# Attention units of a transformer block read in one transfer each: e stored by sign, numerators read with a stride

## The chip, the cores and the metric

The kernel runs on one core of one Trainium2 chip. The metric is device time in microseconds (us) of one execution, lower is better. A core has five engines with queues of their own: PE (TensorE, matrix products; its weight loads are listed as PEld), DVE (VectorE), ACT (ScalarE), POOL (GpSimd) and SP (SyncE, which here only issues transfers). Transfers between device memory (DRAM) and the on-chip memory SBUF run on 16 DMA engines; SP issues most of them, ACT issues one kind. PE writes its results to PSUM banks, 128 partitions of 512 floats.

## The reference

One transformer block on x of 2048 tokens by 1024 features, all in float32:

```python
qkv = x @ wqkv                                  # x after a layer norm; 32 heads of 32
pq = einsum("bhsd,hdf->bhsf", q, w_phi);  pk = einsum("bhsd,hdf->bhsf", k, w_phi)
phi_q = concat([softmax(pq), softmax(-pq)], -1) # 64 features per head; phi_k likewise
kv = einsum("bhsf,bhsd->bhfd", phi_k, v);  z = einsum("bhsf->bhf", phi_k)
num = einsum("bhqf,bhfd->bhqd", phi_q, kv)
den = einsum("bhqf,bhf->bhq", phi_q, z)[..., None] + 1e-6
h = x + (num / den).reshape(B, S, D) @ wo
h2 = h + relu(layernorm(h) @ w1) @ w2           # w1: 1024 x 3584
```

So for every token and head there are 32 exponentials with the sign plus and 32 with the sign minus, called e below.

## The kernel before

**Stages.** The order of all work is written out by hand: a list of PE items (`items`), and for every other step a number (`when(step, f, ...)`), a step being one eighth of an item at first and one quarter later. Each engine carries out its part in the order in which the code issues it. First come keys and values (to about 520 us), with the query projections of tokens 0 to 1023 in between; then the query projections of tokens 1024 to 2047, the attention and the output projection side by side (to about 800 us); then the MLP in a form that needs seven instead of eight block products. Products of matrices are three matmuls each (`mm3`, L182 to L184), since every operand is split in a high and a low part; the weights' split (L125 on ACT, L129 on DVE or POOL) runs beside.

**From the projection to e.** For a tile t of 128 tokens and one half s of the heads, PE leaves pq in a bank. DVE takes the largest and smallest value of each head (L516, L517) and the two differences (L520, L521) into the tile `qe`, 128 tokens by `(a, s, c, f)`: 4 groups of heads, 2 signs, 4 heads, 32 features, 1024 floats. ACT takes the exponential (`q_second`, L525) and stores the tile to the scratch tensor `ed` in DRAM (L527, a transfer on ACT's queue). DVE sums e per head and sign (L533), POOL multiplies sums and inverses to factors `smq` (L543), which SP stores to `smd` for every group of four tiles (`sm_store`, L547).

**Groups and units.** The 16 tiles form four groups of four (`groups`); `place_of` gives a tile's group b and place i in it. For each group there are 8 units, one for each of 8 groups of 4 heads, 32 units in all. A unit is a tile of 128 partitions by 8 x 128 floats (`qe` again in the names of the profile, `xl` for the first six): partitions 32a to 32a + 31 hold 32 tokens t; quarters a = 0, 1 are the signs of tiles i = 0, 1, quarters 2, 3 those of tiles i = 2, 3. The free dimension is `(n, c, f)`: 8 blocks of 32 tokens, 4 heads, 32 features. `at_load` (and, earlier and once more, `early_load` for the first six, whose denominators are made ahead) reads it by `by_quarter` (L551), four transfers of 128 KB on SP's queue, one for each quarter, in pieces of 512 bytes. `sm_load` reads the factors the same way.

**In a unit.** POOL multiplies e by z (L595), DVE sums (L602), ACT copies each quarter's sums to the other sign's quarter (L613), POOL and DVE make the denominator (L617, L618, L621), POOL scales e (L631; L626 for the early units), and DVE turns the tile in blocks of 32 x 32 (`at_turn`, L637): afterwards the partitions are features and the free dimension is `(n, c, t)`, tokens last.

**Numerators.** `at_num` (L650) runs for every second unit: for two units j, two row halves g of 64 partitions (each holds both signs of two tiles) and four heads c, a matmul of `kvL` (64 x 32, stationary) and 256 columns, the turned rows of one head. The eight matmuls of a unit use eight 64 x 32 tiles of the array. f32 matmuls show in the profile as two records each. A row half has its own bank; ACT copies it to the high part of `oT` (L657), DVE takes the low part (L667, `at_low`). `oT` holds for each unit 512 tokens in the order of the tiles and is the stationary operand of the output projection (`wo_item`).

**Two other places the prediction looks at.** `far_scale` (L776), once, at 823 us: 16 small matmuls whose stationary operand is `ident.rearrange("p (t g) -> p g t", g=4)[:, g]`, 32 columns that lie four floats apart. `far_swap` (L781): a DVE turn of 128 x 1024 whose output steps four floats. The transfers `hs<-xin` (L760) store 256 KB in pieces of 512 bytes.

Of the kernel before, what the change touches and what calls it, by code (L numbers as in the profile page):

```python
# [9 lines left out]
F32 = mybir.dt.float32  # L10
# [5 lines left out]
P = 128  # L16
# [124 lines left out]
def kernel(  # L141
# [12 lines left out]
    v, act, pool, pe, sp = nc.vector, nc.scalar, nc.gpsimd, nc.tensor, nc.sync  # L154
# [5 lines left out]
    dram = ctx.enter_context(tc.tile_pool(name="scratch", bufs=1, space=bass.MemoryType.DRAM))  # L160
# [9 lines left out]
    def ac_bank():  # L170
        return psum.tile([P, 512], F32, name="ac", bufs=2)
# [22 lines left out]

    groups = (0, 1, 4, 5), (2, 3, 6, 7), (8, 9, 10, 11), (12, 13, 14, 15)
    place_of = {t: (b, i) for b, tiles in enumerate(groups) for i, t in enumerate(tiles)}
    ed = [dram.tile([8, 4, P, 256], F32, name=f"ed{b}") for b in range(4)]
    smd = [dram.tile([4, P, 64], F32, name=f"smd{b}") for b in range(4)]
    hd = [dram.tile([P, D], F32, name=f"hd{t}") for t in range(NT)]


# [219 lines left out]
    e_of, v_of, phi_of, kv_ps, kd_of = {}, {}, {}, {}, {}  # L421
# [102 lines left out]
    def q_second(s, t):  # L524
        act.activation(e_of[s, t], e_of[s, t], AF.Exp)  # L525
        b, i = place_of[t]
        act.dma_start(ed[b].rearrange("a i p x -> p a i x")[:, 4 * s:4 * s + 4, i, :],  # L527
                      e_of[s, t].rearrange("p a s c f -> p a (s c f)"))

    def q_third(s, t):  # L530
        b, i = place_of[t]
# [12 lines left out]
                               op=ALU.mult)  # L544

    def sm_store(b):
        sp.dma_start(smd[b].rearrange("i p x -> p i x"), smq[:, b % 2].rearrange("p i s n -> p i (s n)"))  # L547

    def by_quarter(dst, src):
        for a in range(4):  # L550
            sp.dma_start(dst[32 * a:32 * (a + 1)],  # L551
                         src[2 * (a // 2):2 * (a // 2) + 2].rearrange("i (n t) (s x) -> s t (i n) x", t=32, s=2)[a % 2])

    def sm_load(b):
        by_quarter(smx[:, b % 2], smd[b])


    e_q, ez_of, tz_of, den_of, ph_of, acc_of, phT_of = {}, {}, {}, {}, {}, {}, {}
# [4 lines left out]
    def at_load(u):  # L563

        e = ap_.tile([P, D], F32, name="qe", bufs=6)
        e_q[u] = e = e.rearrange("p (n x) -> p n x", n=8)
        by_quarter(e, ed[u // 8][u % 8])
# [4 lines left out]
    def early_load(u):  # L572
        e_q[u] = e = xlp.tile([P, D], F32, name="xl").rearrange("p (n x) -> p n x", n=8)
        by_quarter(e, ed[u // 8][u % 8])
# [59 lines left out]
    def at_turn(u):  # L634

        ph = ph_of.pop(u)
        v.transpose(ph, ph)  # L637
        phT_of[u] = ph.rearrange("p (n c t) -> p n c t", n=8, c=4)

    def at_num(u):  # L640


        acc_of[u] = banks = ac_bank(), ac_bank()
        for j in range(2):
            b, q, r = UNITS[u - 1 + j]
            for g in range(2):
                rows = slice(64 * g, 64 * (g + 1))
                for c in range(4):
                    h = 2 * c + r
                    pe.matmul(banks[g][32 * c:32 * (c + 1), 256 * j:256 * (j + 1)],  # L650
                              kvL[rows, 2 * q + h // 4, 32 * (h % 4):32 * (h % 4 + 1)],
                              phT_of[u - 1 + j][rows, :, c, :], start=j == 0, stop=j == 1)
        del phT_of[u - 1], phT_of[u]
        if u % 8 == 1:
            oT[b] = opool[b % 2].tile([P, 2, 8, 512], F32R, name="oT")
        for g in range(2):
            act.activation(at_out(u, 0, g), at_in(banks[g]), AF.Copy)  # L657

    def at_in(ps):
        return ps.rearrange("p (u n) -> p u n", u=2)  # L660

    def at_out(u, part, g):
        return oT[u // 8][:, part, u % 8 - 1:u % 8 + 1, 256 * g:256 * (g + 1)]

    def at_low(u):
        for g, ps in enumerate(acc_of.pop(u)):
            v.tensor_sub(at_out(u, 1, g), at_in(ps), f32(at_out(u, 0, g)))  # L667

    oT, opool = {}, {}
# [277 lines left out]
    def item(gen, *args, keys):  # L947
        items.append((gen, args + (keys,)))
        steps.extend((k,) for k in keys)
        return len(items) - 1  # L950
# [11 lines left out]
    for b, tiles in enumerate(groups):  # L962
        for hf in range(2):

            pairs = b == 0 and hf == 0
            for j in range(0, 4, 2 if pairs else 1):
# [3 lines left out]
                for half in range(2):  # L970
                    n = item(wo_pair, tiles[j:j + 2], hf, half, keys=[("wo", hf, 4 * half + k // 2) for k in range(8)])
# [36 lines left out]
    for t in range(1, NT):  # L1008
        n = t - 1 if t < HT else q_n[1, t - HT] + 1
# [106 lines left out]
    for (sl, t), n in q_n.items():  # L1116
        when(8 * n + 14, q_second, sl, t)
        when(8 * n + 19, q_third, sl, t)
        when(8 * n + 27, q_fourth, sl, t)
        b, i = place_of[t]  # L1120
        if (sl, i) == (1, 3):
            when(8 * n + 34, sm_store, b)
            when(8 * n + (48, 48, 48, 72)[b], sm_load, b)
    for u in range(32):
        start = 8 * (a0 + u) if u >= 8 else 8 * (last_kv + 4) + 19 * u // 2
        slack = 6 if u < 6 else 0

        for step, f, *args in ((-5, at_load), (6, at_sums, 0), (10, at_reduce, 0), (9, at_sums, 1), (12, at_reduce, 1),
                               (14, at_cross), (16, at_den), (18, at_inverse), (20, at_scale), (26, at_turn)):
            if u >= EARLY or f in (at_load, at_scale, at_turn):  # L1130
                when(max(start + step, 8 * (last_kv + 4)), f, u, *args)
        if u % 2:
            when(start + 30 + slack, at_num, u)
            when(start + 32 + slack, at_low, u)
        if u < EARLY:
            start = 8 * (kv_n[1, u // 2, NT - 1] + 4) + (-2, 19)[u % 2]
            for step, f in ((0, early_load), (9, early_sums), (14, early_reduce), (17, at_cross), (20, at_den), (22, early_scale)):
                when(start + step, f, u)
# [73 lines left out]
    for b in range(2):  # L1212
        for m in DOWN:
            n = down_n[b, m, NP - 1] + 1
            name, more = {1: "x1", 5: "x4", 6: "x2", 4: "x3"}.get(m), \
# [109 lines left out]
```

## Time and profile before

| | |
|---|---|
| median of 3 runs | 1880.37 us (1880.06 to 1882.46) |
| the profiled execution | 1877.44 us |
| its span, first to last instruction | 1875.6 us |
| PE busy | 1859.8 us, 99% |
| PE clock granted, mean | 0.999 |
| DVE, ACT, POOL busy | 57%, 41%, 52% |

The profile is of one execution. Rows of groups give line, engine, operation, names as out<-in, the tile of the array for PE, shapes, count, then busy time in us and mean ns of one, then idle time of the engine just before and what ended it. Rows of a timeline start with the start in us and the duration; an x32 is that many instructions merged. Rows of transfers give the count, KB of each and the median us from issue to landing. PEld are weight loads, which overlap with PE; "SPq" and "ACTq" are the sequencers that issue transfers.

### The profile page before, as it was taken

How to read it: one execution, taken by the hardware profiler on the slowest of the kernel's cores; microseconds unless marked ns; L12 is line 12 of the kernel's file. 1: busy time of each engine (PE TensorE's matmuls, PEld its weight loads, DVE VectorE, ACT ScalarE, POOL GpSimd, SP SyncE). 2: the span in 40 equal slices, each digit the busy share in tenths (PEclk: the TensorE clock that was granted, in tenths of full speed). 3: DMA queues.
4: the chain of work that ended last, by engine and by line, in shares of the span. 5: the costliest groups of instructions: out<-in, count | busy, mean ns of one | idle time of the engine just before them, and what ended most of it. 6: DMA issues, size and time to landing. Idle time of an engine off the chain costs nothing.

```text
span 1875.6 us, 29094 instructions
## 1 busy us (share of the span) xinstructions
PE 1859.8 (99%) x10064; PEld 1517.2 (81%) x10064; DVE 1070.5 (57%) x1655; ACT 771.3 (41%) x1379; POOL 981.3 (52%) x991
## 2 busy tenths in 40 slices
PE   9999999999999999999999999999999999999999
PEld 7877788888887777888888888888888888888887
DVE  7787688677689878565555663344433333343333
ACT  5322244233333333255455554444444444444442
POOL 4887745888946989443332222222344444444443
PEclk9999999999999999999999999999999999999999
DMA  7988788666677897887888975666676777777775
GB/s 229 291 290 286 229 295 261 204 196 199 181 217 193 222 224 200 261 283 227 243 265 265 322 260 176 195 192 217 214 230 214 214 220 239 237 215 218 216 215 178
DMA packets 348963, 433.05 MB, mean 231 GB/s; under 512 B 32272, under 2 KB 219664, under 8 KB 348816
## 3 DMA queue, kind: packets, MB, share of 16 engines
q1 hardware_dynamic: 331920, 414.42, 72.6%
q10 hardware_dynamic: 16896, 16.78, 2.7%
q8 instruction: 79, 1.29, 0.3%
q14 instruction: 68, 0.56, 0.1%
HBM read 293.21 MB, written 137.89 MB: 230 GB/s over the span
## 4 chain that ended last, share of the span: by engine, by line
PE 92%; DMA 2%; DVE 2%; POOL 2%; issue 1%; ACT 0%; SPq 0%; DVEq 0%; POOLq 0%; ACTq 0%
PE mm L182 24%; PE mm L183 23%; PE mm L184 23%; PE ac L182 4%; PE ac L184 4%; PE ac L183 4%; PE tp L182 2%; PE tp L184 2%; PE tp L183 2%; PE tp L246 1%; PE ac L465 1%; DMA qe<-ed 1%; POOL qe L631 1%; DMA ed<-qe 1%; POOL ez L595 0%
## 5 line engine op out<-in xcount | busy, mean ns | idle before, releaser
L129 POOL TENSOR_TENSOR w<-raw,w 128x512 fp32r<-128x512 f32 x353 | 470.1, 1334 | 698.6 <-ACT w L125 651.4
L125 ACT ACTIVATE w<-raw 128x512 fp32r<-128x512 f32 x686 | 409.4, 626 | 510.9 <-PE mm L184 239.8
L129 DVE TENSOR_TENSOR w<-raw,w 128x512 fp32r<-128x512 f32 x333 | 271.6, 816 | 515.0 <-ACT w L125 503.4
L182 PE MATMUL mm<-w,xT 128*128 128x512 f32 x768 | 305.4, 398 | 0.0
L183 PE MATMUL mm<-w,xT 128*128 128x512 f32 x768 | 299.8, 390 | 0.4 <-POOL w L401 0.4
L184 PE MATMUL mm<-w,xT 128*128 128x512 f32 x768 | 299.2, 390 | 0.0
L184 PE MATMUL mm<-hT,w 128*128 128x512 f32 x672 | 261.4, 389 | 0.0
L182 PE MATMUL mm<-hT,w 128*128 128x512 f32 x672 | 261.4, 389 | 0.0
L183 PE MATMUL mm<-hT,w 128*128 128x512 f32 x672 | 261.4, 389 | 0.0
L182 PEld LDWEIGHTS mm<-w,xT 128*128 128x128 f32 x768 | 144.1, 188 | 34.8 <-issue 3.7
L184 PEld LDWEIGHTS mm<-w,xT 128*128 128x128 f32 x768 | 144.2, 188 | 30.7
L363 POOL TENSOR_TENSOR b<-b 128x256 f32<-128x256 f32 x176 | 143.5, 815 | 47.6 <-DMA b<-in_w_dram 31.9
L183 PEld LDWEIGHTS mm<-w,xT 128*128 128x128 f32 x768 | 144.3, 188 | 29.2 <-POOL w L401 1.0
L182 PE MATMUL mm<-w 128*128 128x512 f32 x392 | 152.5, 389 | 0.0
L183 PE MATMUL mm<-w 128*128 128x512 f32 x392 | 152.5, 389 | 0.0
L184 PE MATMUL mm<-w 128*128 128x512 f32 x392 | 152.5, 389 | 0.0
L183 PEld LDWEIGHTS mm<-hT,w 128*128 128x128 f32 x672 | 126.1, 188 | 26.3
L184 PEld LDWEIGHTS mm<-hT,w 128*128 128x128 f32 x672 | 126.1, 188 | 26.2
L182 PEld LDWEIGHTS mm<-hT,w 128*128 128x128 f32 x672 | 126.1, 188 | 26.1
L183 PEld LDWEIGHTS mm<-w 128*128 128x128 f32 x392 | 73.6, 188 | 15.3
L184 PEld LDWEIGHTS mm<-w 128*128 128x128 f32 x392 | 73.6, 188 | 15.3
L182 PEld LDWEIGHTS mm<-w 128*128 128x128 f32 x392 | 73.6, 188 | 15.3
(173 smaller groups left out, 3119.5 us busy)
## 6 DMA issues: line engine op xcount, KB each, us to landing
raw<-t SPq DMA_DIRECT2D x224, 256.0 KB, 3.8
raw<-ad SPq DMA_DIRECT2D x196, 256.0 KB, 3.0
raw<-in_w_dram SPq DMA_DIRECT2D x168, 256.0 KB, 3.1
ad<-c SPq DMA_DIRECT2D x112, 256.0 KB, 3.6
b<-in_w_dram SPq DMA_DIRECT2D x44, 512.0 KB, 6.0
t<-b SPq DMA_DIRECT2D x44, 512.0 KB, 4.8
ad<-s SPq DMA_DIRECT2D x84, 256.0 KB, 3.8
ed<-qe ACTq DMA_DIRECT2D x32, 512.0 KB, 4.3
```

Source lines behind the costliest of these rows:

```text
L125: nc.scalar.activation(w[:, 0, :], raw[1], AF.Copy)
L129: eng.tensor_tensor(out=w[:, 1, :], in0=raw[1], in1=w[:, 0, :].bitcast(F32), op=ALU.subtract)
L182: pe.matmul(ps, a_hi, b_hi, start=first, stop=False, skip_group_check=more)
L183: pe.matmul(ps, a_hi, b_lo, start=False, stop=False, skip_group_check=more)
L184: pe.matmul(ps, a_lo, b_hi, start=False, stop=last, skip_group_check=more)
L246: pe.transpose(pt[:, k, :], xn[:, (4 * j + k) * P:(4 * j + k + 1) * P], ident)
L363: pool.tensor_tensor(out=tsum[*u, *out], in0=tsum[*u, *a], in1=tsum[*u, *b], op=ALU.subtract)
L465: pe.matmul(kv_ps[s][g][32 * i:32 * (i + 1), 0:64], vt[:, 32 * h:32 * (h + 1)], phi[:, 64 * h:64 * (h + 1)], start=first, stop=last)
L631: pool.tensor_tensor(out=e, in0=e, in1=sd[:, :, None].to_broadcast([P, 32, 32]), op=ALU.mult)
```

## The change

The scratch tensors get another layout, so that a unit's rows lie in DRAM as the unit's partitions want them: the row is `(g, s, t)`, half, sign and 32 tokens, and in it follow four tokens n and 128 floats each. Token 4t + n of a tile now stands in partition t, where before it was token 32n + t.

- The store of e (`q_second`) becomes two transfers, one for each sign, of 256 KB each. Each partition writes 4 pieces of 512 bytes a transfer, where it wrote 4 pieces of 1 KB in one.
- The store of the factors (`sm_store`) writes pieces of 128 bytes instead of 256.
- `by_quarter` becomes one transfer over all 128 partitions, two pieces of 2 KB for each: a unit is read by one issue of 512 KB. The read of the factors likewise has pieces of 512 bytes.
- The turned rows are now `(i, n, c, t)` with tokens in the order `(i, t, n)`. `at_num` reads them in that order: four columns n that lie 128 floats apart, then the next t. The number and shape of the matmuls are the same.
- The copies to `oT` write pieces of 128 floats instead of 256, since a row half g now holds the tiles i = g and 2 + g.

All that stands below `q_second` in the file moves by one or two lines in the new kernel (L551 becomes L552).

On SP, in the output projection of the second group, a unit's load stands as one row with four issues (`hd` and `xh` are results and inputs of the output projection):

```order
L714 DMA hd_90<-xh 128x512
L674 DMA xh<-in_x_dram 128x512
L551 DMA qe<-ed_82 32x8x128 x4
L714 DMA hd_91<-xh 128x512
L674 DMA xh<-in_x_dram 128x512
L551 DMA qe<-ed_82 32x8x128 x4
```

The same place in the changed kernel:

```order
L714 DMA hd_90<-xh 128x512
L674 DMA xh<-in_x_dram 128x512
L552 DMA qe<-ed_82 128x2x512
L714 DMA hd_91<-xh 128x512
L674 DMA xh<-in_x_dram 128x512
L552 DMA qe<-ed_82 128x2x512
```

The place of the load among the others is the same; three of its four issues are gone. On ACT, at the last query tiles, before:

```order
L525 ACTIVATE qe<-qe 128x1024
L527 DMA ed_83<-qe 128x4x256
L613 ACTIVATE qden<-qtz 32x32 x4
L657 ACTIVATE oT<-ac 128x2x256 x2
L125 ACTIVATE w<-raw 128x512 x3
```

and after:

```order
L525 ACTIVATE qe<-qe 128x1024
L529 DMA ed_83<-qe 128x4x128 x2
L613 ACTIVATE qden<-qtz 32x32 x4
L657 ACTIVATE oT<-ac 128x4x128 x2
L125 ACTIVATE w<-raw 128x512 x3
```

A second issue stands between the exponential and the copies of a unit's sums. On PE, DVE and POOL no instruction changes its place.

```diff
-    ed = [dram.tile([8, 4, P, 256], F32, name=f"ed{b}") for b in range(4)]
-    smd = [dram.tile([4, P, 64], F32, name=f"smd{b}") for b in range(4)]
+    ed = [dram.tile([8, 2, P, 512], F32, name=f"ed{b}") for b in range(4)]
+    smd = [dram.tile([2, P, P], F32, name=f"smd{b}") for b in range(4)]
...
     def q_second(s, t):
         act.activation(e_of[s, t], e_of[s, t], AF.Exp)
         b, i = place_of[t]
-        act.dma_start(ed[b].rearrange("a i p x -> p a i x")[:, 4 * s:4 * s + 4, i, :],
-                      e_of[s, t].rearrange("p a s c f -> p a (s c f)"))
+        dst = ed[b].rearrange("a i (g s t) (n x) -> s (i g) (t n) a x", g=2, s=2, n=4)
+        for sd in range(2):
+            act.dma_start(dst[sd, i, :, 4 * s:4 * s + 4], e_of[s, t].rearrange("p a s c f -> s p a (c f)")[sd])
...
     def sm_store(b):
-        sp.dma_start(smd[b].rearrange("i p x -> p i x"), smq[:, b % 2].rearrange("p i s n -> p i (s n)"))
+        sp.dma_start(smd[b].rearrange("i (g s t) (n x) -> (t n) (i g s) x", g=2, s=2, n=4),
+                     smq[:, b % 2].rearrange("p i s n -> p (i s) n"))
 
     def by_quarter(dst, src):
-        for a in range(4):
-            sp.dma_start(dst[32 * a:32 * (a + 1)],
-                         src[2 * (a // 2):2 * (a // 2) + 2].rearrange("i (n t) (s x) -> s t (i n) x", t=32, s=2)[a % 2])
+        sp.dma_start(dst.rearrange("p (i n) x -> p i (n x)", i=2), src.rearrange("i q x -> q i x"))
...
         v.transpose(ph, ph)
-        phT_of[u] = ph.rearrange("p (n c t) -> p n c t", n=8, c=4)
+        phT_of[u] = ph.rearrange("p (i n c t) -> p c i t n", i=2, n=4, c=4)
...
                               kvL[rows, 2 * q + h // 4, 32 * (h % 4):32 * (h % 4 + 1)],
-                              phT_of[u - 1 + j][rows, :, c, :], start=j == 0, stop=j == 1)
+                              phT_of[u - 1 + j][rows, c], start=j == 0, stop=j == 1)
...
     def at_in(ps):
-        return ps.rearrange("p (u n) -> p u n", u=2)
+        return ps.rearrange("p (u i n) -> p u i n", u=2, i=2)
 
     def at_out(u, part, g):
-        return oT[u // 8][:, part, u % 8 - 1:u % 8 + 1, 256 * g:256 * (g + 1)]
+        return oT[u // 8][:, part, u % 8 - 1:u % 8 + 1, :].rearrange("p u (i g n) -> p u i g n", i=2, g=2)[:, :, :, g]
```

## The prediction

> **What bounds the kernel now.** I read the page first, then who PE waited for, then a table of stretches over the attention stage, then that stage's matmuls one by one.
>
> ```profile
> span 1875.6 us, 29094 instructions
> PE 1859.8 (99%) x10064; PEld 1517.2 (81%) x10064; DVE 1070.5 (57%) x1655; ACT 771.3 (41%) x1379; POOL 981.3 (52%) x991
> ...
> PE ac L650 <- DVE qe L637: 4.0, 4, 1.7
> PE mm L183 <- DVE w L129: 1.8, 1, 1.8
> ...
> PE tp L246 <- ACT xin L248: 1.5, 1, 1.5
> PE ac L650 <- POOL ez L595: 1.3, 1, 1.3
> ...
> 540.00:600.00 60.00, 58.74 (x365) 45.86 (x364) 57.18 (x84) 22.91 (x40) 39.70 (x48) 1.00 0.70 193
> 600.00:660.00 60.00, 55.43 (x338) 41.40 (x337) 47.67 (x70) 20.66 (x60) 56.44 (x61) 0.97 0.91 234
> 660.00:760.00 100.00, 96.82 (x661) 74.80 (x661) 77.92 (x118) 34.40 (x86) 83.39 (x98) 1.00 0.83 216
> 610.00:615.00 5.00, 4.59 (x37) 2.92 (x26) 2.59 (x4) 2.65 (x6) 3.77 (x8) 0.66 0.75 163
> ```
>
> PE is the bound: 1859.8 of 1875.6 us. What PE does longer adds to the time one for one; what other engines or DMA queues do shorter can give back no more than PE now waits. A row of waits has the total in us, the count, the longest. A row of stretches has, after the stretch's length, the busy time of PE, PEld, DVE, ACT and POOL, then the granted clock, DMA share and GB/s. Nearly all that this change touches lies from 540 to 760 us. PE idles there 1.26 + 4.57 + 3.18 = 9.0 us (length less PE busy), and near 612 us, after several of these waits, the granted clock is 0.66 for one piece of 5 us, worth 5 x 0.34 = 1.7 us. So 10.7 us is all that faster transfers could bring. DVE is busy 57.18 of 60 us in the first piece and POOL 56.44 of 60 in the second: the waits are largely those engines' work, which the change leaves as it is.
>
> **The numerator matmuls (at_num), read with a stride.** They are what PE itself does differently.
>
> ```profile
> L650 PE MATMUL ac<-qe,kvL x512: 372/376/631, 550.5 to 758.2; 64*32 64x256 f32 x171
> L488 PE MATMUL tp<-zacc,ones 128*128 128x512 f32 x8 | 4.1, 590 | 0.0
> 650.96 1.09 PE L650 MATMUL ac<-qe,kvL 64*32 64x256 f32 x32
> ```
>
> There are 512 records of 256 columns, in 16 bursts of 32 (the timeline row is one, 1.09 us). A burst uses eight 64x32 tiles of the array, so each tile runs 32 / 8 = 4 records in a row. Between f32 matmuls of 256 and 512 columns lie 590 - 376 = 214 ns, so a column costs 214 / 256 = 0.84 ns, and a tile's four records stream for 4 x 256 x 0.84 = 0.86 us: the stream, not a fixed cost, fills the burst. Before, a record reads runs of 32 neighbouring floats; after, neighbouring columns are 128 floats (512 bytes) apart. No matmul of this trace reads its moving operand so, but two other operations step through SBUF:
>
> ```profile
> L776 PEld LDWEIGHTS tp<-scx,ident 128*32 128x32 f32 x32 | 0.6, 154 | 0.4 <-issue 0.4
> L465 PEld LDWEIGHTS ac<-kphi,vt 128*32 128x32 f32 x1024 | 15.4, 110 | 8.5 <-issue 6.8 <-DVE ksm L443 0.7 <-DVE kphi L446 0.4
> L488 PEld LDWEIGHTS tp<-zacc,ones 128*128 128x128 f32 x8 | 1.5, 188 | 0.3
> 823.10 0.58 PEld L776 LDWEIGHTS tp<-scx,ident 128*32 128x32 f32 x32 [0.35 <-issue]
> L781 DVE STREAM_TRANSPOSE xin<-xin 128x1024 f32<-128x1024 f32 x4 | 8.0, 2005 | 0.1
> L637 DVE STREAM_TRANSPOSE qe<-qe 128x1024 f32<-128x1024 f32 x32 | 39.3, 1227 | 4.6 <-POOL qe L631 2.7 <-DMA ed<-qe 1.8
> ```
>
> L776 (far_scale) loads 32 columns of `ident` that lie four floats apart, L465 the same shape with neighbours: 154 against 110 ns, so 44 / 32 = 1.4 ns more a column. Neighbouring columns cost (188 - 110) / 96 = 0.81 ns, close to the 0.84 of a matmul column, so the two streams ask SBUF for floats at one pace. DVE's transpose at L781 writes floats four apart: (2005 - 1227) / 1024 = 0.76 ns more for each.
>
> Bounds for a burst. Low end, 0: the stream's pace of one f32 column per 0.84 ns may be slow enough to hide the step; a gain is excluded, since the same columns pass. By DVE's row: 4 x 256 x 0.76 = 0.78 us a burst, 12.4 us for 16. By the weight row: 4 x 256 x 1.4 = 1.43 us, 22.9 us for 16. High end: the four column tiles on the same 64 partitions take turns, each column having its own 0.84 ns: 16 x 256 x 0.84 = 3.44 us instead of 0.86, 2.58 more a burst, 41.3 us for 16. The 32 strided loads of L776 took 0.58 us for 32 x 32 columns, 0.57 ns a column over four column tiles, which speaks against strict turns. I take the weight row: same engine, a read, the same pace, several tiles at once: **+22.9 us**.
>
> [...]
>
> **The copies out of the banks.** ACT L657 and DVE L667 keep 512 elements, written now in pieces of 128 instead of 256. The nearest pair, whole rows against pieces of 32:
>
> ```profile
> L707 DVE TENSOR_TENSOR xh<-mm,xh 128x512 f32<-128x512 f32 x16 | 11.0, 686 | 17.5 <-DMA hs<-s4l 6.6 <-PE mm L184 5.7 <-DMA hd<-xh 5.2
> L704 DVE TENSOR_TENSOR xh<-mm,xh 128x512 f32<-128x512 f32 x16 | 10.7, 679 | 1.3 <-PE mm L184 1.3
> ```
>
> 7 ns each, 32 times, 0.2 us on an engine that isn't PE: nothing either way. The turn itself (L637) is untouched.
>
> **The transfers.**
>
> ```profile
> ed<-qe ACTq DMA_DIRECT2D x32, 512.0 KB, 4.3
> qe<-ed SPq DMA_DIRECT2D x128, 128.0 KB, 4.6
> xin<-in_x_dram SPq DMA_DIRECT2D x19, 512.0 KB, 5.9
> hd<-xh SPq DMA_DIRECT2D x32, 256.0 KB, 4.4
> hs<-xin SPq DMA_DIRECT2D x32, 256.0 KB, 4.1
> smd<-smq SPq DMA_DIRECT2D x4, 128.0 KB, 3.4
> ...
> L527 ACTq DMA_DIRECT2D ed<-qe x32: 366/367/418, 226.5 to 606.0; - x32
> 689.79 1.90 SPq L551 DMA_DIRECT2D qe<-ed  x4
> 561.01 24.54 SPq L551 DMA_DIRECT2D qe<-ed  x20
> 567.43 2.55 POOL L595 TENSOR_TENSOR ez<-qe,zb 128x512 f32<-128x512 f32 x2 [6.28 <-DMA qe<-ed]
> 584.19 1.92 POOL L631 TENSOR_TENSOR qe<-qe,qden 128x1024 f32<-128x1024 f32 x1 [3.38 <-DVE qden L621]
> 731.74 0.76 PE L650 MATMUL ac<-qe,kvL 64*32 64x256 f32 x16 [1.67 <-DVE qe L637]
> ```
>
> Loads: a unit's four issues take SP 1.90 us, one takes about 1.90 / 4 = 0.48, so SP's queue gains 1.4 us a unit, 45 us over 32 units. The data comes hardly earlier: the last quarter lands 3 x 0.48 + 4.6 = 6.0 us after the first issue, a 512 KB load 5.9 us. Queued behind the loads on SP are the weights of wo and the rows of x; the stretch of 24.54 us for 20 issues is SP held back by buffers that aren't free yet, which one issue in place of four doesn't change. POOL's wait of 6.28 us at 567 is for such a load; but a little later POOL waits for DVE (3.38 us before 584), which is busy nearly throughout. So of the load side I count at most what PE's waits hold, and without the stride I would count 3 us of the 10.7, about the wait at 731.74 (1.67) and that for L248 (1.5), which end a stretch where SP, DMA and POOL are all late.
>
> Stores: 32 more issues on ACT, 32 x 0.367 = 11.7 us, half of them after 510 us, beside 20 to 23 us of ACT work in 60. Pieces become 512 bytes: `hs<-xin` has such pieces (256 KB, 4.1 us), `hd<-xh` pieces of 2 KB (4.4 us), so the second half lands about 0.4 us later than the one store did. Bounds for the time: 0, and 0.4 us for each of the 16 tiles stored after 510 us, 6.4 us, if each were on the path. I take 0: none of PE's waits above is put down to a store. The factors' store goes to 128-byte pieces, 1024 for 512: at worst twice its 3.4 us, four times, with SP waiting before the load; 4 x 3.4 = 13.6 us of SP's queue, less than the 45 it gains; 0 on PE.
>
> **What comes back.** A PE that is later meets fewer waits.
>
> ```profile
> 564.72 1.09 PE L650 MATMUL ac<-qe,kvL 64*32 64x256 f32 x32
> 578.88 1.09 PE L650 MATMUL ac<-qe,kvL 64*32 64x256 f32 x32
> 590.89 0.76 PE L650 MATMUL ac<-qe,kvL 64*32 64x256 f32 x16 [1.26 <-POOL ez L595]
> ```
>
> Three bursts lie before the first wait (the first at 550.5, by the row of L650 above), 3 x 1.43 = 4.3 us against 1.26; a burst comes about every 13 us and adds 1.43, and PE's idle time to 660 is 1.26 + 4.57 = 5.8 us in all, so the lag is ahead of the waits. All 10.7 us could go; but DVE's sums of the output projection wait for PE in its queue, ahead of transposes that PE needs, so I count **-8**. Sum: +22.9 - 8 = +14.9 us. The profiled execution took 1877.44 us (span 1875.6); the median of the runs is 1880.37, 2.9 above. On the median: 1880.4 + 14.9 = 1895 us.
>
> **Rivals.** A (mine): the step costs between DVE's row and somewhat above the weight row: +12.4 less 7, to +33 less 9: 1886 to 1904.
> B, faster: the step is free and SP's shorter queue lets POOL and DVE run ahead. For it: the load that POOL waits 6.28 us for, and 45 us of SP. Against it: L776's 154 ns, DVE and POOL full. It gives -4 to -10.7, about 1874. It decides if a burst grows by less than (10.7 - 4) / 16 = 0.4 us.
> C, no change to measure: the step is free or nearly so, and the waits stay DVE's and POOL's: about 1879.
> D: the four column tiles take turns, or 512 bytes are worse than 16: +41.3 - 10.7 = +31, 1911, and beyond if a turn costs more than 0.84 ns. For it: four streams from the same partitions. Against it: the 0.57 ns a column of L776.
>
> **Chances.** A 0.48, B 0.16, C 0.13, D 0.23. A change of 0.2% (3.8 us, 1876.6 to 1884.1) is about what a measurement of this kernel can tell from none; so faster 0.16, within 0.13, slower 0.71. The range reaches down through C into the upper part of B and up past D's 1911: 1876 to 1914; left out are about two thirds of B (0.1) and D's tail (0.08). A's own range is 1886 to 1904.
>
> **What the profile after would show.** The records of at_num at about 376 + 256 x 1.4 = 730 ns instead of 376, a burst at about 2.5 us instead of 1.09; under B and C still 376; under D a burst near 3.6 us. PE idle from 540 on falls from 9.0 us to some 3. `qe<-ed` has 32 issues of 512 KB near 6 us, `ed<-qe` 64 of 256 KB. I am wrong if the records stay at 376 ns: then the weight row was no measure for the moving operand; or if PE's idle time grows although the bursts are longer: then a late store or load is a new wait.

## The result, and the profile after

The changed kernel takes 1884.99 us (median of 20 runs, 1883.82 to 1885.87), the kernel before 1881.45 us beside it (20 runs, 1879.71 to 1884.92): ratio 1.0016, 95% interval 1.0009 to 1.0023. It is slower, by 3.5 us where +14.9 were forecast; the profiled execution took 1884.29 us.

The page's head, the waits of PE, the table of stretches (after the length: PE, PEld, DVE, ACT, POOL, clock, DMA share, GB/s), and from the page of DMA issues the transfers of e, all of the changed kernel:

```profile
span 1882.5 us, 28853 instructions
PE 1871.4 (99%) x10064; PEld 1516.4 (81%) x10064; DVE 1067.8 (57%) x1655; ACT 770.9 (41%) x1379; POOL 979.9 (52%) x991
...
PE tp L246 <- ACT xn L239: 2.3, 1, 2.3
PE ac L650 <- DVE qe L637: 1.9, 1, 1.9
PE tp L1244 <- POOL ones L1240: 1.6, 1, 1.6
PE mm L183 <- DVE w L129: 1.1, 1, 1.1
...
540.00:600.00 60.00, 60.00 (x355) 44.33 (x354) 56.12 (x84) 22.64 (x40) 37.67 (x47) 1.00 0.58 180
600.00:660.00 60.00, 57.00 (x337) 40.14 (x336) 47.67 (x66) 19.80 (x56) 55.44 (x58) 1.00 0.76 243
660.00:760.00 100.00, 100.00 (x623) 73.74 (x622) 76.81 (x117) 34.27 (x88) 84.73 (x98) 1.00 0.66 206
...
ed<-qe ACTq DMA_DIRECT2D x64, 256.0 KB, 3.9
qe<-ed SPq DMA_DIRECT2D x32, 512.0 KB, 5.0
```

The numerators after, all 512 records (min/median/max in ns) and one burst:

```profile
L650 PE MATMUL ac<-qe,kvL x512: 610/627/707, 551.0 to 764.7; 64*32 64x256 f32 x171
592.38 2.08 PE L650 MATMUL ac<-qe,kvL 64*32 64x256 f32 x32
```

A record takes 627 ns where it took 376, (627 - 376) / 256 = 0.98 ns more a column, and a burst 2.07 us where it took 1.09: 16 x 0.98 = **15.7 us** more of PE for 16 whole bursts. PE's busy time in these matmuls, from 540 to 770 us, before and then after (PE, PEld, clock, DMA share, GB/s):

```profile
540.00:770.00 230.00, 19.86 (x512) 7.76 (x512) 0.99 0.82 219
540.00:770.00 230.00, 33.75 (x512) 8.50 (x512) 1.00 0.68 213
```

It grew by 33.75 - 19.86 = 13.9 us only. Before, five of the 16 bursts came in two halves with a wait of PE between them, and two halves take longer than a whole (0.66 + 0.76 us against 1.09 at the full clock); after, one does. So 15.7 us is the price of the stride by itself, and 13.9 us is what PE did longer here. PE's idle time from 540 to 760 us fell from 9.0 to 3.0 us (60 - 57.00), and the piece with the clock at 0.66 is gone (clock 1.00 in all three stretches), 1.7 us more. Between the two profiles that is 15.7 - 6.0 - 1.7 = +8.0 us, or +6.2 with 13.9; the spans differ by 6.9. But the medians differ by 3.5 only. So the result asks three things: what sets the 15.7 us, where the other waits went, and why the profile before showed fewer of them than the median run has.

### The profile page after: what moved, and what is told of

It is laid out like the page before. It is cut to its first block, busy times and chain, and to the rows that moved or that the text cites. A ratio compares the mean times of both kernels' runs of the same rounds, so it can differ in the third digit from the quotient of the medians.

```text
span 1882.5 us, 28853 instructions
## 1 busy us (share of the span) xinstructions
PE 1871.4 (99%) x10064; PEld 1516.4 (81%) x10064; DVE 1067.8 (57%) x1655; ACT 770.9 (41%) x1379; POOL 979.9 (52%) x991
## 4 chain that ended last, share of the span: by engine, by line
PE 97%; POOL 1%; DVE 1%; issue 0%; DMA 0%; ACT 0%; SPq 0%; DVEq 0%; POOLq 0%
PE mm L182 25%; PE mm L183 25%; PE mm L184 25%; PE ac L182 4%; PE ac L184 4%; PE ac L183 4%; PE tp L184 2%; PE tp L183 2%; PE tp L182 2%; PE ac L650 2%; PE tp L246 1%; PE ac L465 1%; POOL ez L595 0%; PE tp L291 0%; POOL w L129 0%
## 5 line engine op out<-in xcount | busy, mean ns | idle before, releaser
L454 POOL TENSOR_TENSOR zacc<-zacc,kphi 128x512 f32<-128x512 f32 x60 | 80.7, 1345 | 10.1 <-DVE kphi L446 10.1
L182 PEld LDWEIGHTS mm<-w 128*128 128x128 f32 x392 | 73.6, 188 | 15.3
L183 PEld LDWEIGHTS mm<-w 128*128 128x128 f32 x392 | 73.6, 188 | 15.3
```

Source lines behind the costliest of these rows:

```text
L182: pe.matmul(ps, a_hi, b_hi, start=first, stop=False, skip_group_check=more)
L183: pe.matmul(ps, a_hi, b_lo, start=False, stop=False, skip_group_check=more)
L454: pool.tensor_tensor(out=zacc[s], in0=zacc[s], in1=phi_of[key], op=ALU.add)
```

## Experiments

### The kernel before once more

Nothing is edited.

> The kernel before, unchanged, for a second profile, since the first one is of an execution 2.3 us faster than the fastest of 20 others. If the spread lies in the waits of the attention, as both theories need, PE idles here more than 9.0 us from 540 to 760 us, or the clock is granted lower there for longer; if it lies elsewhere, the difference between the two profiles sits ahead of 540 us or behind 760 us.

It took 1884.62 us, 7.2 us of span more than the first profile. The head of its page, the same stretches, and the three pieces of 5 us with a lower clock:

```profile
span 1882.8 us, 29094 instructions
PE 1861.2 (99%) x10064; PEld 1518.3 (81%) x10064; DVE 1069.0 (57%) x1655; ACT 771.5 (41%) x1379; POOL 982.8 (52%) x991
...
540.00:600.00 60.00, 58.74 (x365) 45.90 (x364) 57.18 (x84) 22.92 (x40) 39.55 (x48) 1.00 0.69 192
600.00:660.00 60.00, 54.59 (x336) 41.04 (x335) 47.40 (x69) 20.57 (x60) 56.17 (x59) 0.97 0.96 235
660.00:760.00 100.00, 92.85 (x605) 71.62 (x604) 73.05 (x114) 33.31 (x84) 80.71 (x94) 0.97 0.80 203
...
625.00:630.00 5.00, 3.96 (x24) 2.57 (x25) 3.27 (x5) 2.11 (x4) 4.92 (x6) 0.66 0.58 165
735.00:740.00 5.00, 3.78 (x22) 2.48 (x23) 4.50 (x9) 2.17 (x7) 3.10 (x5) 0.53 0.74 186
740.00:745.00 5.00, 5.00 (x19) 3.96 (x18) 3.34 (x5) 2.33 (x3) 4.74 (x8) 0.79 0.44 147
```

PE idles 1.26 + 5.41 + 7.15 = 13.8 us here, and the clock costs 5 x 0.34 + 5 x 0.47 + 5 x 0.21 = 5.1 us: 18.9 us in the prediction's terms, where the first profile had 10.7. These terms are upper bounds, since they charge the clock also for the time in which PE idles. By the heads of the two pages, PE idles 1882.8 - 1861.2 = 21.6 us over the whole span against 1875.6 - 1859.8 = 15.8: 5.8 us more, 4.8 of them from 540 to 760 us; and it is busy 1.4 us longer. Together that is the 7.2 us between the spans. So these two executions differ mostly by what the attention stage waits, and the profile of the prediction showed one of the shortest: 1877.44 us, where the fastest of 20 others took 1879.71.

### Stride alone, transfers alone

Stride alone, on the kernel before:

```diff
-        phT_of[u] = ph.rearrange("p (n c t) -> p n c t", n=8, c=4)
+        phT_of[u] = ph.rearrange("p (i n c t) -> p c i t n", i=2, n=4, c=4)
...
-                              phT_of[u - 1 + j][rows, :, c, :], start=j == 0, stop=j == 1)
+                              phT_of[u - 1 + j][rows, c], start=j == 0, stop=j == 1)
```

> The kernel before with one edit: at_num reads the turned rows in the order (i, t, n), neighbouring columns 128 floats apart, as the change does; stores and loads of e are those of before. The tokens of each tile then leave the attention in another order and are not put back, so the result is of rows exchanged within a tile; the amount of work is the same. Both theories: records of at_num at 627 ns and bursts near 2.07 us, as after the change, 16 x 0.98 = 15.7 us more of PE. Theory L (lag): a later PE meets fewer waits, whatever the transfers do, and the new transfers give nothing themselves: about the time after the change, 1885 us, PE idle from 540 to 760 us near 3 us. Theory T (transfers): the waits went because units arrive earlier and SP is free: here they stay in part, 1889 to 1897 us, PE idle 5 to 9 us.

Transfers alone, on the changed kernel:

```diff
-        phT_of[u] = ph.rearrange("p (i n c t) -> p c i t n", i=2, n=4, c=4)
+        phT_of[u] = ph.rearrange("p (i n c t) -> p c i n t", i=2, n=4, c=4)
```

> The changed kernel with one edit: at_num reads the turned rows in the order (i, n, t), runs of 32 neighbouring floats as before; all stores and loads of e are the new ones. The tokens of each tile leave the attention in another order and are not put back, so rows are exchanged within a tile; the amount of work is the same. Both theories: records of at_num back at 376 ns, bursts at 1.09 us. Theory L: no gain from the transfers, within 2 us of the kernel before, PE idle from 540 to 760 us near 9 us again. Theory T: the waits are gone without the longer bursts, 5 to 10 us faster than before, 1871 to 1876 us, PE idle near 3 us.

| | time | before beside it | ratio, interval |
|---|---|---|---|
| stride alone | 1886.70 us (7 runs) | 1880.35 us (17) | 1.0030, 1.0019 to 1.0041 |
| transfers alone | 1876.14 us (11 runs) | 1880.35 us (17) | 0.9978, 0.9969 to 0.9987 |

Neither theory held as stated. With the stride alone the records are at 624 ns and the time grows by 6.3 us, not 15.7: a later PE swallows 15.7 - 6.3 = 9.4 us of its waits whatever the transfers do (8.1 by PE's busy time in these matmuls, which grew by 14.4 us here), more than theory T allowed. And the transfers by themselves make the kernel faster, by 4.2 us, where theory L saw nothing. Together the two give +2.1, near the +3.5 measured. With the longer bursts the transfers are worth 6.3 - 3.5 = 2.8 us, though the intervals of these two ratios overlap. The profile of the transfers alone still shows PE idle for 7.9 us from 540 to 760 us, not the 3 of theory T; the first profile of the kernel before had 9.0, the second 13.8.

### What sets the price of the stride

One head of four with the strided read, on the kernel before:

```diff
+        phT_of[u] = ph.rearrange("p (i n c t) -> p c i t n", i=2, n=4, c=4), ph.rearrange("p (i n c t) -> p c i n t", i=2, n=4, c=4)
...
+                              phT_of[u - 1 + j][c > 0][rows, c], start=j == 0, stop=j == 1)
```

> The kernel before, with the strided read for one of the four heads of a unit only (c = 0); the other three read runs of 32. Rows of these heads leave in another order. If a strided stream is slow by itself, whatever the other column tiles read, the records of c = 0 take 627 ns and the others 376 to 400 unless they queue behind it, and a burst is again near 2.0 us. If the four column tiles share a port and it is their sum that is slow, a fourth of the columns being strided costs about a fourth: records near 440 ns, a burst near 1.35 us.

The records of the numerators and one burst:

```profile
L650 PE MATMUL ac<-qe,kvL x512: 376/376/630, 550.9 to 764.9; 64*32 64x256 f32 x171
580.97 1.96 PE L650 MATMUL ac<-qe,kvL 64*32 64x256 f32 x32
```

The minimum and the median stay at 376 ns, a fourth of the records, the strided ones, take 610 to 630, and the burst takes 1.96 us of the 2.07: one strided stream of four costs nearly all. So it isn't the sum of the four column tiles' streams that is slow; one strided stream by itself takes 0.84 + 0.98 = 1.8 ns a column, an estimate from the 0.84 of the prediction and the 627 and 376 ns of a record.

Two other steps, on the kernel before, w = 4 and w = 2; with 4 each column lies in other 16 bytes than the one before it, with 2 two in a row come from the same 16:

```diff
+        phT_of[u] = ph.rearrange("p (n c u w) -> p c n w u", n=8, c=4, w=4)
```

> The kernel before, at_num reading columns that lie 4 floats (16 bytes) apart in runs of eight, instead of neighbours; rows leave in another order. If the price comes with every column that lies in another 16-byte line than the one before it, records are 627 ns as with 512 bytes. If it grows with the distance, they lie between 376 and 627 ns. [...]

> The kernel before, at_num reading columns 2 floats (8 bytes) apart in runs of sixteen; rows leave in another order. [...] If the price comes with a new line for each column, records are at 376 ns here; if it comes with any step that isn't 1, they are at 620 ns as with 4 floats and with 128.

Their records, the step of 4 floats first, then the step of 2:

```profile
L650 PE MATMUL ac<-qe,kvL x512: 589/619/656, 550.9 to 769.0; 64*32 64x256 f32 x171
```

```profile
L650 PE MATMUL ac<-qe,kvL x512: 372/395/633, 550.5 to 759.3; 64*32 64x256 f32 x171
```

A step of 16 bytes costs as much as one of 512 (619 and 627 ns); a step of 8 bytes costs 19 ns a record (395). That fits a price for each column that needs another 16 bytes than the one before it; a limit on the step itself, somewhere above 8 and up to 16 bytes, would show the same. No run tells the two apart, and none shows the lines that the two expectations speak of. (The three kernels ran once each: 1884.41 us with one head strided, 1888.56 with the step of 4 floats, 1878.51 with the step of 2.)

### Which part of the transfers gives the gain

Three versions of the transfers alone. Four issues of 32 partitions, in pieces of 2 KB:

```diff
-        sp.dma_start(dst.rearrange("p (i n) x -> p i (n x)", i=2), src.rearrange("i q x -> q i x"))
+        for a in range(4):
+            rows = slice(32 * a, 32 * (a + 1))
+            sp.dma_start(dst[rows].rearrange("p (i n) x -> p i (n x)", i=2), src.rearrange("i q x -> q i x")[rows])
```

> The transfers alone (contiguous numerators, rows exchanged within a tile), but a unit is read by four issues of 32 partitions each, still in pieces of 2 KB. Theory I (issues): the gain is SP's queue, one issue for four; it goes, and the time is that before, within 2 us. Theory P (pieces): the gain is the DMA engines' time for long pieces; it stays, about 4 us faster than before, DMA share from 600 to 660 us near 0.75 as with the transfers alone, where it was 0.91 before.

One issue, in pieces of 512 bytes:

```diff
+        sp.dma_start(dst.rearrange("p (n i) x -> p n i x", i=2), src.rearrange("i q (n x) -> q n i x", n=4))
```

> The transfers alone, a unit read by one issue over 128 partitions, but in eight pieces of 512 bytes for each partition instead of two of 2 KB (the blocks of a unit come in another order, so rows are exchanged between two tiles; the amount of work is the same). Theory I: one issue is what counts; the gain of 4 us stays. Theory P: the gain goes, DMA share from 600 to 660 us back near 0.9.

Four issues over 128 partitions:

```diff
+        for i in range(2):
+            for j in range(2):
+                sp.dma_start(dst.rearrange("p (i m) x -> p i (m x)", i=4)[:, 2 * i + j], src[i].rearrange("q (m x) -> q m x", m=2)[:, j])
```

> The transfers alone (contiguous numerators, rows exchanged within a tile), a unit read by four issues again, but each over all 128 partitions (two pieces of 512 bytes for each partition) instead of 32 partitions. Theory I (issues): four issues on SP take the gain away as four narrow ones did: the time before, within 2 us. Theory W (width): what costs is a transfer that ends on 32 partitions, which keeps others back on the way to SBUF; four wide issues keep most of the gain, 3 to 6 us faster than before, and the DMA queues move over 300 GB/s from 690 to 700 us, as with one wide issue (333), where four narrow ones moved 247 to 263.

| a unit's read | time | before beside it | ratio, interval | GB/s, 690 to 700 us |
|---|---|---|---|---|
| 1 wide, 2 KB (transfers alone) | 1876.14 us | 1880.35 us | 0.9978, 0.9969 to 0.9987 | 333 |
| 1 wide, 512 bytes | 1876.73 us | 1882.66 us | 0.9968, 0.9956 to 0.9981 | 322 |
| 4 wide, 512 bytes | 1876.58 us | 1880.71 us | 0.9974, 0.9964 to 0.9984 | 298 |
| 4 of 32 partitions, 2 KB | 1882.01 us | 1882.66 us | 0.9994, 0.9985 to 1.0003 | 247 |

The last column is from the stretch 690 to 700 us of each. That of the transfers alone, then that of the four narrow issues:

```profile
690.00:700.00 10.00, 10.00 (x58) 8.00 (x43) 8.69 (x16) 2.91 (x10) 6.89 (x8) 1.00 0.93 333
```

```profile
690.00:700.00 10.00, 10.00 (x73) 7.65 (x72) 6.32 (x13) 2.00 (x6) 6.67 (x9) 1.00 1.00 247
```

Theory P fell with the second row of the table: short pieces keep the gain. Theory I fell with the third: four issues keep it too, if each ends on all 128 partitions. Four wide issues moved 298 GB/s, where theory W asked for over 300. Only the transfers that end on 32 partitions lose the gain, with the DMA engines as busy (1.00) and fewer bytes moved from 690 to 700 us. The last column speaks for that stretch alone, in one profile of each: from 600 to 660 us one wide issue in short pieces and four narrow ones moved 241 and 236 GB/s at the same DMA share of 0.83. Why a transfer that ends on 32 partitions keeps the gain away, no run shows.

### Where the narrow transfers hurt

On DVE, the kernel before once more first (the run above), then the transfers alone, around 695 us:

```profile
693.21 1.27 DVE L222 BATCH_NORM_STATS2 st<-xin 128x6 f32<-128x512 f32 x2
694.52 0.21 DVE L224 BATCH_NORM_AGGREGATE mv<-st 128x2 f32<-128x12 f32 x1
697.23 1.29 DVE L222 BATCH_NORM_STATS2 st<-xin 128x6 f32<-128x512 f32 x2 [2.50 <-DMA xin<-hd]
698.55 0.21 DVE L224 BATCH_NORM_AGGREGATE mv<-st 128x2 f32<-128x12 f32 x1
698.68 1.20 DVE L637 STREAM_TRANSPOSE qe<-qe 128x1024 f32<-128x1024 f32 x1
```

```profile
694.34 1.23 DVE L222 BATCH_NORM_STATS2 st<-xin 128x6 f32<-128x512 f32 x2
695.60 0.21 DVE L224 BATCH_NORM_AGGREGATE mv<-st 128x2 f32<-128x12 f32 x1
695.73 1.19 DVE L637 STREAM_TRANSPOSE qe<-qe 128x1024 f32<-128x1024 f32 x1
```

The second layer norm's statistics (L222, `ln_pair` stage 1) wait on DVE for the rows of h (`xin<-hd`), whose transfer runs among the units' loads. The turn of a unit (L637), its denominator and the next sums are queued behind them on DVE. With one wide load the rows are there in time. The second profile of the kernel before shows the whole chain 40 us later, where it ends in PE's longest wait of the stage:

```profile
733.53 1.29 DVE L222 BATCH_NORM_STATS2 st<-xin 128x6 f32<-128x512 f32 x2 [2.45 <-DMA xin<-hd]
734.98 1.19 DVE L637 STREAM_TRANSPOSE qe<-qe 128x1024 f32<-128x1024 f32 x1
736.22 1.20 PE L650 MATMUL ac<-qe,kvL 64*32 64x256 f32 x16 [4.54 <-DVE qe L637]
```

The experiment takes this wait away without any new transfer, on the kernel before:

```diff
-    NEAR = 0, 9, 12, 17, 24, 24, 27, 27, 30, 36
+    NEAR = 0, 12, 13, 17, 24, 24, 27, 27, 30, 36
```

> The kernel before with its own transfers and numerators, and one other edit: the statistics of the second layer norm (L222) and the step after them are issued three and one steps later, so that DVE turns the unit (L637) and sums the next ones (L602) ahead of them. If the wait through which the transfers act is DVE's for the rows of h (xin from hd) with the turns queued behind it, this takes it away without any new transfer: 3 to 6 us faster than before. If the transfers act through the units' own arrival, it does nothing, within 2 us.

It takes 1874.06 us (5 runs) against 1880.71: ratio 0.9964, interval 0.9952 to 0.9977. Its stretch, and DVE at the same place:

```profile
660.00:760.00 100.00, 100.00 (x678) 78.26 (x677) 80.15 (x126) 34.40 (x86) 83.92 (x103) 1.00 0.93 236
...
693.16 1.23 DVE L637 STREAM_TRANSPOSE qe<-qe 128x1024 f32<-128x1024 f32 x1
694.31 0.31 DVE L621 RECIPROCAL qden<-qden 128x32 f32<-128x32 f32 x1
694.54 1.21 DVE L602 TENSOR_REDUCE qtz<-ez 128x16 f32<-128x512 f32 x2
695.68 1.27 DVE L222 BATCH_NORM_STATS2 st<-xin 128x6 f32<-128x512 f32 x2
```

PE doesn't idle from 660 to 760 us, with the DMA share higher than before (0.93 against 0.83): the wait was that of DVE's queue. The first-named reason holds; the units' own arrival isn't needed for a gain of this size. All profiles together, with the second load of the rows of h around 690 us (from issue to landing) and all of DVE's waits for such rows at L222 (L223 in the two versions with x turned, described below):

| a unit's read | profiles | the load lands after | DVE's waits at L222 |
|---|---|---|---|
| 4 of 32 partitions | 7 | 5.1 to 7.5 us | 0.6 to 6.2 us |
| 4 of 32 partitions, statistics late | 1 | 8.0 us | 0.6 us |
| 4 wide | 1 | 6.2 us | 1.5 us |
| 1 wide | 4 | 3.6 to 5.3 us | 0 to 0.3 us |
| 1 wide, statistics late | 1 | 3.5 us | 0 us |

With the statistics late the rows of h land as late as ever and DVE hardly waits for them. One thing stays open: with four wide issues the load lands as in the first profile of the kernel before (6.2 us), DVE waits 1.5 us and PE idles 2.5 us from 660 to 760, yet the time is 4.1 us shorter. So the ratios, not that profile, carry the verdict on width, and that the gain of four wide issues comes through L222 isn't shown. The spread of the runs is worth a look too. Versions with narrow transfers, numerators read without the stride and the statistics where they were spread by 4.3 to 6.2 us; all others with 5 runs or more spread by 1.2 to 2.6. That fits the longest waits being what goes.

### Without the stride, and both edits

The changed kernel's transfers, with a second copy of x whose rows are turned inside each tile, so that the tokens come out of runs of 32 in their own order:

```diff
+        "xq": x.reshape(NT, 4, 32, D).transpose(0, 2, 1, 3).reshape(S, D),
...
-        return [x[t * P:(t + 1) * P, :]]
+        return [xq[t * P:(t + 1) * P, :]]
...
+        phT_of[u] = ph.rearrange("p (i n c t) -> p c i n t", i=2, n=4, c=4)
```

> The transfers of the changed kernel without its strided read, made whole: the inputs carry a second copy of x whose rows are turned inside each tile (row 4t + n holds token 32n + t), only the layer norms ahead of the projections read it, and at_num then reads runs of 32 floats and finds the tokens in their own order. Nothing is left out. If what the transfers alone gave (ratio 0.9978) is the transfers and not the order of the rows, this has the same time: 4 us faster than before, about 1876 us, records of at_num at 376 ns. If the exchanged rows had saved something, it falls back to the time before.

> The version with one wide transfer for each unit and x turned in its tiles (correct, nothing left out), with the statistics issued later as well. If both edits remove the same wait, it is no faster than either, ratio near 0.997; if the statistics still hold DVE up with the new transfers, up to 3 us more, ratio near 0.995.

The first takes 1876.28 us (6 runs) against 1882.66: ratio 0.9968, interval 0.9956 to 0.9980. With the statistics late as well (the same edit of `NEAR`) it is 1874.88 us (5 runs) against 1880.71: 0.9968, 0.9955 to 0.9980. Both edits together are no faster than either, as was expected if they remove the same wait. The simplest of the faster versions is the kernel before with the two numbers of `NEAR` changed.

## Why the prediction was wrong

**PE as the bound, and that its extra time is paid one for one less what it gives back:** right, and the direction with it. The records grew, the waits shrank.

**The stride, +22.9 us:** right mechanism, wrong size, and the larger of the two misses: 22.9 - 15.7 = 7.2 us. It measured 0.98 ns a column, between DVE's row (0.76 ns, 12.4 us) and the weight row (1.4 ns, 22.9 us). The weight row was taken because of "same engine, a read, the same pace"; it was the upper of the two. Why a strided column costs a weight load 1.4 ns and a moving operand 0.98 no run shows. Rival D's turns were wrong: one strided stream of four costs as much as four.

**The waits that come back, -8 us:** this failed in size too. 15.7 - 3.5 = 12.2 us came back (10.4 if PE's own 13.9 us are taken). The two misses have the same sign, 7.2 + 4.2 = 11.4 us, and that is the way from +14.9 to +3.5. The bound of 10.7 us, "all that faster transfers could bring", was read from one profile as if it were the kernel's; a second profile of the same kernel shows 18.9 us in the same terms. The text noted that this execution lay 2.9 us below the median and put it in as a constant; by the two profiles such a difference is mostly waits (5.8 of 7.2 us), and waits are what a later PE swallows. The reason for counting 8 of 10.7, that DVE's sums would hold up transposes, left no sign: PE idles 3.0 us in the stage after the change.

**The transfers, 3 us without the stride:** 4.2 us measured, near by luck, since it came by another path than any that was named. SP's queue (45 us of issues) and the landing of a unit (6.0 against 5.9 us) were priced; four wide issues keep the gain with as many issues as before, and late statistics give as much with the units landing as before. What mattered is that DVE waits for the rows of h, whose load lands late among narrow transfers, with PE's next turns queued behind. The rows were in the first trace:

```profile
695.61 1.29 DVE L222 BATCH_NORM_STATS2 st<-xin 128x6 f32<-128x512 f32 x2 [1.36 <-DMA xin<-hd]
698.64 1.92 POOL L631 TENSOR_TENSOR qe<-qe,qden 128x1024 f32<-128x1024 f32 x1 [4.23 <-DVE qden L621]
```

The prediction read another of POOL's waits on DVE, that before 584 us, where DVE works without a gap, and put all of them down to DVE being full.

**Stores, factors, copies out of the banks:** 0 on PE, as forecast; no wait of PE after is put down to a store. The store's two halves land in 3.9 us each.

**Range and chances:** 1884.99 us is within 1876 to 1914, below the 1886 to 1904 of case A; the case that came is A's mechanism with C's size, since 15.7 us and 12.2 us nearly cancel. That the range holds it is luck: its lower part was made for B and C, whose mechanisms didn't come.

## What to carry to other kernels

Before pricing what a change can give back, take the waits from more than one execution, or compare the profiled execution's time with the spread of the runs: here the runs spread by 5 us, two profiles differed by 5.8 us of PE's idle time, and these waits were the first thing that each change moved. When a transfer is reshaped, look at which other transfers run beside it and who waits for those in which queue; here the gain lay in a load that the change doesn't touch, and two numbers in the order of DVE's work gave as much. For an f32 matmul's moving operand a step of 8 bytes between columns was nearly free here, one of 16 was not: 395 and 619 ns a record, against 376 for neighbours.

## What was not expected of the hardware

A strided f32 stream into TensorE was slow by itself: with one of four column tiles strided the burst takes 1.96 us of the 2.07 that all four take. A step of 512 bytes cost hardly more than one of 16: 619 ns at 16, 627 at 512, 395 at 8, 376 for neighbours. And a lower clock came after a long wait of PE: in the second profile of the kernel before, the wait of 4.54 us that ends at 736.22 is followed by granted clocks of 0.53 and 0.79 in two pieces of 5 us, worth up to 5 x 0.47 + 5 x 0.21 = 3.4 us. The wait of 1.87 us in the changed kernel (at 627.42 us) was followed by none: the clock is 1.00 in all its stretches.
